# Attention scores on four 64x64 tiles of the array, and the gate sums moved four steps forward

## The chip, the cores and the metric

The kernel runs on one core of a Trainium2 chip. A core has a matrix engine (TensorE; PE in the profile, with PEld for its weight loads), a vector engine (VectorE, DVE), a scalar engine (ScalarE, ACT), a general engine (GpSimd, POOL) and a queue engine that issues transfers (SyncE, SP). Each has its own instruction stream, and they wait for each other by semaphores. Matrix products read the on-chip memory and write to accumulator banks (PSUM, eight banks of 128 partitions x 512 f32), which VectorE and ScalarE read. The metric is device time in microseconds (us), the median of several executions.

## The reference

Multi-query attention (8 batches, 16 heads, 384 tokens, head size 64, one key and value head) is followed by a mixture of experts over the 3072 tokens: each token picks one of 4 groups and then one of 4 experts in that group.

```python
scores = scale * np.matmul(q, k.transpose(0, 1, 3, 2))
scores = scores - np.max(scores, axis=-1, keepdims=True)
attn = np.exp(scores)
attn = attn / (np.sum(attn, axis=-1, keepdims=True) + 1e-09)
x = np.matmul(attn, v)            # as (3072, 1024) for what follows
...
g_idx = np.argmax(x @ w_group, axis=1)       # g_w: its softmax weight
e_idx = np.argmax(xg @ w_expert[g], axis=1)  # e_w: its softmax weight
h = np.maximum(xg[mask_e] @ w1[g, e], 0.0)
out[tok_idx] = (g_w * e_w)[:, None] * (h @ w2[g, e])
```

## The kernel before

**Tiling and loop.** The attention is cut into 24 tiles t (batch b = t // 3, token tile j = t % 3 of 128 tokens). A tile has eight units, one for each pair of heads, and the main loop takes two units in each of its 96 steps i, four steps to a tile (p = i % 4). The program's order in this loop is the order on each engine's queue; nothing reorders it later.

**A step.** `scores` (L194 to L202) computes for a unit the 128 x 384 scores of two heads: the transposed queries `qt` hold one head in partitions 0 to 63 and the other in 64 to 127, the transposed keys `kt` hold the same keys in both halves, and for each head one f32 matmul with 64 rows and 128 weight columns writes one bank of the unit's PSUM tile `s` (two banks; two such tiles exist, so the unit after the next one needs the bank back). `soft` (L204) takes the negated row maximum on VectorE (`nmx`, L209, one instruction for both heads) and the exponentials with their row sums on ScalarE (L212, one per head). Then TensorE has other work: in steps p = 0 and 1 a share of the expert's matmuls (`advance`, L553; first layer L465, second layer L479), in steps p = 2 and 3 half each of the previous tile's product with V (`pv`, L238, matmul at L249). `pv` cuts the array into 32-row by 64-column tiles: for each of 12 key blocks and four row groups, two heads, with heads as the column half (`tile_position=(32 * i, h * D)`). VectorE goes on with the 32x32 block transposes of the probabilities of two steps before (`transp`, L231), `norm` (L221) takes the reciprocals of the row sums on VectorE (L223) and multiplies the probabilities by them on GpSimd (L227): this is the scaling. In some steps VectorE also transposes queries (`q_blocks`, L186) and keys (`k_blocks`, L165).

**Slots of a step.** Further work is entered by `at(step, where, function)` (L564) and run at named places of that step (L634 to L660): "m0", "m1" and "m2" around TensorE's other work, "v" after it, "w" after the transposes and right before `norm`, "e" right after `norm`, "g" at the step's end.

**The gate.** For each batch, the logits are computed in steps 12b+8 and 12b+16 (`logits`, L266). In step 12b+9 the first token tile chooses the expert that gets the whole batch (`gate_first`, `gate_choose` with the matmul of L333, `gate_score` from L342, `gate_pick` from L362), and the loads of its weights are issued from GpSimd (`load_main`, L445). `gate_masks` (L303, step 12b+17) makes the choice of every token and the exponentials `g_ex`. `gate_values` (L400) then sums these exponentials and takes the reciprocals on VectorE (L402, L404) and makes the weights on GpSimd with four small products (L407, L411, L419, L423). `gate_selected` (L429) reduces them to one factor per token (`gsel`, L433, VectorE). The expert of batch b (`main_expert`, L517) is spread over the steps from 12b+17 on, and reads `gsel` when its second layer's results are scaled (L497), first in step 12b+24.

**After the loop** (L664 to L732) the last tile's product, the last batch's expert and a second expert for that batch follow; the steps of the last batch that lie beyond 95 are run there by hand (`run(i + 10, "w")` and so on, with i = 96). A loop over further experts, as many as remain, comes last (L734).

Of the kernel before, what the change touches and what calls it, by code (L numbers as in the profile page):

```python
# [12 lines left out]
P = 128  # L13
# [6 lines left out]
def kernel(  # L20
# [11 lines left out]
    nc = tc.nc  # L32
    B, H, S, D = q.shape
# [160 lines left out]
    def scores(u):  # L194
        b, j, c = units[u]
        qt, kt = st["qt", u // 8, c // 4], st["kt", b]
        s = ps_s.tile([P, 2, 512], FP32, tag="s")
        cc = c % 4
        for h in range(2):
            r = slice(h * D, (h + 1) * D)  # L200
            nc.tensor.matmul(out=s[:, h, 0:S], lhsT=qt[r, ts(cc, P)], rhs=kt[r, :], start=True, stop=True)  # L201
        st["s", u] = s  # L202

    def soft(us, between):  # L204
# [359 lines left out]
    def at(slot, where, fn, *args):  # L564
        later.setdefault((slot, where), []).append((fn, args))

    def run(slot, where):
        for fn, args in later.pop((slot, where), []):
            fn(*args)
# [4 lines left out]
    for b in range(B):  # L574
        s0 = SB * b
        for x, j0, j1 in ((s0 + 8, 0, 1), (s0 + 16, 1, ST)):
            at(x, "m2", logits, b, j0, j1)
            at(x + 1, "v", logits_out, b, j0, j1)
        at(s0 + 9, "v", gate_first, b)
        at(s0 + 9, "m2", gate_choose, b)  # L580
        at(s0 + 9, "w", gate_score, b)
        at(s0 + 9, "w", gate_pick, b)
        at(s0 + 9, "g", load_main, b, 0)
        at(s0 + (10 if b == B - 1 else 9), "g", load_main, b, 1)
        at(s0 + 16, "g", keep_xb, b)
        at(s0 + 17, "v", gate_masks, b)
        x = s0 + (19 if b == B - 2 else 22)
        at(x, "w", gate_values, b)
        at(x + 1, "w", gate_selected, b)
        if b == B - 1:  # L590
            at(s0 + 13, "w", gate_pick_second, b)
        if b + 1 < B:
            at(s0 + 2, "g", load_k, b + 1)
            at(s0 + 4, "g", load_v, b + 1)
            at(s0 + 7, "g", scale_k, b + 1)
            at(s0 + 8, "e", k_blocks, b + 1)
# [17 lines left out]
    for g in range(G):  # L614
        nc.sync.dma_start(
            out=wge[:, :, G + g * Eg:G + (g + 1) * Eg],
# [17 lines left out]
    for i in range(NSL):  # L634
        t, p = i // 4, i % 4
        if i >= SB + 5 and (i - 5) % SB == 0:
            pending.append(main_expert((i - 5) // SB - 1, lambda k: True))
        us = (2 * i, 2 * i + 1)
        for u in us:
            scores(u)  # L640
        run(i, "s")
        soft(us, lambda: run(i, "b"))
        if p < 2:
            run(i, "m0")
            advance(1)
            run(i, "m1")
            advance(2 if p == 1 and t % ST > 0 else 1)
        elif t > 0:
            pv(t - 1, (p - 2) * NB // 2, (p - 1) * NB // 2)
        run(i, "v")  # L650
        run(i, "m2")
        if i >= 2:
            transp(2 * i - 4)
            transp(2 * i - 3)
        run(i, "w")
        norm(us)
        run(i, "e")
        if p == 3 and t > 0:
            pv_out(t - 1)
        run(i, "g")  # L660
# [3 lines left out]
    b = B - 1  # L664
    i = NSL
# [30 lines left out]
        out=low, in_=low, pattern=[[-1, P]], compare_op=ALU.is_gt, fill=0.0, base=0, channel_multiplier=1  # L696
# [17 lines left out]
        out=sel[:], in0=iop, scalar1=pcum[:, 0:1], scalar2=pw[:, 0:1], op0=ALU.is_equal, op1=ALU.mult  # L714
# [10 lines left out]
    nsum = pool.tile([P, 1], FP32, tag="r_ns", bufs=1)  # L725
    nc.vector.tensor_reduce(out=nsum[:], in_=fl, axis=AX.X, op=ALU.add)
    nc.vector.tensor_copy(out=lsi[:, NP:NP + 1], in_=nsum[:])
    run(i + 10, "w")
    run(i + 11, "w")
    assert not later  # L730

    advance(1000)  # L732
# [2 lines left out]
    with tc.For_i(0, n_rem, 1) as it:  # L735
        free.clear()
        e = nc.gpsimd.value_load(lse[0:1, ds(it, 1)], min_val=0, max_val=GE - 1)
# [4 lines left out]
            out=xr[:].rearrange("p c t -> p (c t)"), in_=xb_dram[ds(bi, 1)].rearrange("o p c -> (o p) c")  # L742
# [43 lines left out]
```

## Time and profile before

| | us |
|---|---|
| median of 3 runs | 533.39 |
| lowest and highest run | 532.93, 533.71 |
| the profiled execution's own time | 532.0 |
| its span on the core | 530.6 |
| TensorE busy in the span | 504.5 |
| VectorE busy | 416.0 |
| ScalarE busy | 319.6 |
| GpSimd busy | 284.5 |

The granted clock of TensorE was 0.99 in the mean. The rows that the prediction quotes are of four kinds. The page's first part gives each engine's busy time, its share of the span and its instructions. The page's chain follows the work that ended last back from the end, and gives the share of the span by engine and by line. A timeline row has start and length in us, engine, line, operation, written and read tiles, shape of the tile on the array (rows * columns), sizes and count; a row can merge several instructions that follow each other, and in brackets stands the idle time of the engine before it and what ended it ("issue" means that the profile shows nothing it waited for). A list of durations has a line's instructions with the shortest, median and longest in ns. An f32 matmul leaves two matmul records and two weight loads.

### The profile page before, as it was taken

To read this page: it belongs to the slowest core of one execution; us is meant where nothing else is said; L and a number is where in the kernel's file an instruction comes from. 1 tells how busy PE (TensorE), PEld (TensorE's weight loads), DVE (VectorE), ACT (ScalarE), POOL (GpSimd) and SP (SyncE) were. 2 spreads that over 40 slices of the span, in tenths; PEclk is the share of its full clock that TensorE was granted. 3 is DMA by queue.
4 is the path that set the end of the run, shared out by engine and by line. 5 is a ranking of instruction groups with operands and counts; after the bars stand their busy time and mean duration, and the time that the engine had idled before them with its cause. 6 is when DMAs were issued, how large, how long until landed. Compare 5 with 4: busy or idle time off the path is not lost.

```text
span 530.6 us, 18457 instructions
## 1 busy us (share of the span) xinstructions
PE 504.5 (95%) x7470; PEld 283.0 (53%) x7470; DVE 416.0 (78%) x751; ACT 319.6 (60%) x997; POOL 284.5 (54%) x505
## 2 busy tenths in 40 slices
PE   7787899999999999999999999999999999999993
PEld 3254456545565556546655556545664555655451
DVE  3889988998799879987979878987899888914221
ACT  3776776676576667577666666676757666623210
POOL 1555965575458546675349456665458546704000
PEclk9799999999999999999999999999999999999998
DMA  8521996499937993599837993699739950599923
GB/s 112 118 40 43 178 242 159 75 191 246 249 76 124 225 267 89 98 210 252 209 72 134 230 262 76 117 218 241 192 72 172 236 162 3 84 234 259 212 57 94
DMA packets 65607, 83.96 MB, mean 158 GB/s; under 512 B 21232, under 2 KB 40688, under 8 KB 65520
## 3 DMA queue, kind: packets, MB, share of 16 engines
q0 software_dynamic: 19008, 37.75, 39.7%
q1 hardware_dynamic: 45024, 44.65, 33.2%
q8 instruction: 60, 0.98, 0.7%
q10 hardware_dynamic: 1488, 0.36, 0.4%
q14 instruction: 27, 0.22, 0.1%
HBM read 101.61 MB, written 18.87 MB: 227 GB/s over the span
## 4 chain that ended last, share of the span: by engine, by line
PE 84%; DVE 8%; ACT 5%; issue 2%; ACTq 0%; DVEq 0%
PE s L201 22%; PE x L249 22%; PE x L465 14%; PE x L479 12%; PE sb L479 6%; ACT pr L212 5%; PE sb L465 4%; DVE nmx L209 4%; PE x L272 2%; DVE ring L233 2%; DVE qt L191 1%; PE x L98 1%; DVE ohs_all L365 0%; DVE rinv L223 0%; DVE im L367 0%
## 5 line engine op out<-in xcount | busy, mean ns | idle before, releaser
L227 POOL TENSOR_SCALAR pr<-pr,rinv 128x384 f32<-128x384 f32 x384 | 217.1, 583 | 159.7 <-DVE rinv L223 159.7
L212 ACT ACTIVATE pr<-s,nmx 128x384 f32<-128x384 f32 x384 | 217.7, 579 | 139.5 <-DVE nmx L209 134.2
L209 DVE TENSOR_REDUCE nmx<-s 128x2 f32<-128x768 f32 x192 | 174.4, 947 | 50.8 <-PE s L201 50.4
L233 DVE STREAM_TRANSPOSE ring<-pr 128x768 f32<-128x768 f32 x192 | 175.3, 952 | 0.0
L201 PE MATMUL s<-kt,qt 64*128 64x384 f32 x768 | 157.1, 521 | 12.2 <-ACT pr L212 12.0
L249 PE MATMUL x<-ring,v_sb 32*64 32x256 f32 x4608 | 139.5, 379 | 1.6 <-issue 1.5
L249 PEld LDWEIGHTS x<-ring,v_sb 32*64 32x64 f32 x4608 | 102.1, 131 | 43.2 <-issue 24.7
L201 PEld LDWEIGHTS s<-kt,qt 64*128 64x128 f32 x768 | 65.4, 188 | 74.8 <-ACT pr L212 40.0
L465 PEld LDWEIGHTS <-w 128*128 128x128 bf16 x576 | 54.5, 98 | 46.0 <-issue 11.4
L212 ACT ACTIVATION_READ_ACCUMULATOR pr<-s,nmx 128x1 f32 x384 | 77.8, 203 | 0.0
L465 PE MATMUL x<-xb,w 128*128 128x384 bf16 x448 | 76.5, 327 | 0.0
L479 PEld LDWEIGHTS <-h_t 128*128 128x128 bf16 x432 | 40.6, 98 | 56.6 <-issue 10.6
L479 PE MATMUL x<-w,h_t 128*128 128x512 bf16 x288 | 65.3, 380 | 0.0
L263 ACT COPY xt<-x 128x256 f32<-128x256 f32 x96 | 29.0, 386 | 7.3 <-PE x L249 7.3
L479 PE MATMUL sb<-w,h_t 128*128 128x512 bf16 x144 | 31.8, 379 | 0.0
L264 POOL CAST xb<-xt 128x1024 bf16<-128x1024 f32 x24 | 24.8, 1033 | 12.8 <-ACT xt L263 12.8
L471 ACT ACTIVATE h_t<-x 128x384 bf16<-128x384 f32 x56 | 25.4, 502 | 6.1 <-PE x L465 3.3
L440 POOL DMA_DIRECT2D w<-in_moe_w_dram x36 | 27.9, 787 | 2.0 <-issue 2.0
L497 ACT ACTIVATE y<-x,gsel 128x512 f32<-128x512 f32 x36 | 25.0, 693 | 3.9 <-PE x L479 3.9
L191 DVE STREAM_TRANSPOSE qt<-q_sb 128x512 f32<-128x512 f32 x38 | 26.1, 688 | 0.0
L465 PE MATMUL sb<-xb,w 128*128 128x384 bf16 x128 | 21.4, 326 | 0.0
L223 DVE RECIPROCAL rinv<-ssum 128x4 f32<-128x4 f32 x96 | 13.6, 141 | 3.1 <-ACT pr L212 3.1
(85 smaller groups left out, 138.3 us busy)
## 6 DMA issues: line engine op xcount, KB each, us to landing
w<-in_moe_w_dram POOLq DMA_DIRECT2D x36, 1024.0 KB, 18.1
q_sb<-in_q_dram SPq DMA_DIRECT2D x76, 224.0 KB, 6.2
out_dram<-y SPq DMA_DIRECT2D x84, 128.0 KB, 6.4
xb_scratch<-xb SPq DMA_DIRECT2D x8, 768.0 KB, 4.4
v_sb<-in_v_dram SPq DMA_DIRECT2D x32, 96.0 KB, 3.5
kk<-in_k_dram SPq DMA_DIRECT2D x28, 92.0 KB, 3.7
q_sb<-in_q_dram SPq DMA_DIRECT2D x16, 128.0 KB, 3.5
out_dram<-y SPq DMA_DIRECT2D x24, 64.0 KB, 1.7
```

What stands on the lines that cost most here:

```text
L191: nc.vector.transpose(out=qt[:].rearrange("p (x d) -> p x d", d=32), in_=q_sb[:, :, 0:32])
L201: nc.tensor.matmul(out=s[:, h, 0:S], lhsT=qt[r, ts(cc, P)], rhs=kt[r, :], start=True, stop=True)
L209: nc.vector.tensor_reduce(out=nmx[:], in_=s[:, :, 0:S], axis=AX.X, op=ALU.max, negate=True)
L212: nc.scalar.activation(out=pr[:, h, :], in_=s[:, h, 0:S], func=ACTF.Exp, bias=nmx[:, h:h + 1], scale=1.0, accum_out=ssum[:, k, h:h + 1],)
L227: nc.gpsimd.tensor_scalar(out=pr, in0=pr, scalar1=rinv[:, k, h:h + 1], scalar2=1.0, op0=ALU.mult, op1=ALU.mult)
L233: nc.vector.transpose(out=ring[:, (u // 4) % 3, u % 4].rearrange("p h s -> p (h s)"), in_=st.pop(("pr", u))[:].rearrange("p h s -> p (h s)"),)
L249: nc.tensor.matmul(out=o[i][h * D:(h + 1) * D, 0:2 * P].rearrange("d (g c q) -> d g c q", g=2, c=4), lhsT=v_sb[r, n, :], rhs=ring[r, a:z + ...
L263: nc.scalar.copy(out=xt[:, :, ts(i, 32)], in_=o[:, 0:2 * P].rearrange("p (c q) -> p c q", c=KO))
L440: nc.gpsimd.dma_start(out=w[:, o:o + 4, :], in_=(w1f, w2f)[n][ds(e, 1), :, o:o + 4, :].rearrange("o p c f -> (o p) c f"))
L465: nc.tensor.matmul(out=hp[:, 0:S], lhsT=w1[:, ko, ts(fc, P)], rhs=xb[:, ko, :], start=(ko == 0), stop=(ko == KO - 1))
L471: nc.scalar.activation(out=h_t[:, fc, :], in_=hp[:, 0:S], func=ACTF.Relu)
L479: nc.tensor.matmul(out=yp, lhsT=h_t[:, fo, ts(j, P)], rhs=w2[:, fo, ts(nh, 512)], start=(fo == 0), stop=(fo == FO - 1),)
```

## The change

The score matmul of each head is cut by tokens into two of 64 weight columns each, with the array position written out: four tiles of 64 rows by 64 columns, one for each head and each half of the 128 tokens. They write the same banks as before, the token halves into partitions 0 to 63 and 64 to 127.

`gate_values` moves from slot "w" of step 12b+22 (12b+19 for the last batch but one) to slot "e" of step 12b+18, so from ahead of `norm` to behind it and four steps (one step) forward. `gate_selected` moves from step 12b+23 (12b+20) to step 12b+22 (12b+19), its slot "w" unchanged. After the loop, the last batch's two calls follow the same order as before under other names.

```diff
         for h in range(2):
             r = slice(h * D, (h + 1) * D)
-            nc.tensor.matmul(out=s[:, h, 0:S], lhsT=qt[r, ts(cc, P)], rhs=kt[r, :], start=True, stop=True)
+            for m in range(2):
+                nc.tensor.matmul(
+                    out=s[m * D:(m + 1) * D, h, 0:S], lhsT=qt[r, ts(2 * cc + m, D)], rhs=kt[r, :],
+                    start=True, stop=True, tile_position=(h * D, m * D),
+                )
         st["s", u] = s
...
-        x = s0 + (19 if b == B - 2 else 22)
-        at(x, "w", gate_values, b)
-        at(x + 1, "w", gate_selected, b)
+        x = s0 + 18
+        at(x, "e", gate_values, b)
+        at(s0 + (19 if b == B - 2 else 22), "w", gate_selected, b)
...
+    run(i + 6, "e")
     run(i + 10, "w")
-    run(i + 11, "w")
     assert not later
```

## The prediction

> **What bounds the kernel now.** I read the page first: busy shares, then the chain that ended last.
>
> ```profile
> span 530.6 us, 18457 instructions
> PE 504.5 (95%) x7470; PEld 283.0 (53%) x7470; DVE 416.0 (78%) x751; ACT 319.6 (60%) x997; POOL 284.5 (54%) x505
> ...
> PE 84%; DVE 8%; ACT 5%; issue 2%; ACTq 0%; DVEq 0%
> PE s L201 22%; PE x L249 22%; PE x L465 14%; PE x L479 12%; PE sb L479 6%; ACT pr L212 5%; PE sb L465 4%; DVE nmx L209 4%; PE x L272 2%; DVE ring L233 2%; DVE qt L191 1%; PE x L98 1%; DVE ohs_all L365 0%; DVE rinv L223 0%; DVE im L367 0%
> ```
>
> A chain that is TensorE for 84% says that TensorE's own sequence sets the end, and the scores of L201, which the change rewrites, hold 22% of it. Next the timeline of one steady slot, a step of the main loop (here step 43, whose second half is a quarter of the products with V):
>
> ```profile
> 202.91 1.56 PE L201 MATMUL s<-kt,qt 64*128 64x384 f32 x8
> 203.87 1.82 DVE L209 TENSOR_REDUCE nmx<-s 128x2 f32<-128x768 f32 x2 [0.61 <-PE s L201]
> 204.40 2.85 PE L249 MATMUL x<-ring,v_sb 32*64 32x256 f32 x96
> 204.92 0.58 ACT L212 ACTIVATE pr<-s,nmx 128x384 f32<-128x384 f32 x1 [1.88 <-DVE nmx L209]
> 205.61 1.83 DVE L233 STREAM_TRANSPOSE ring<-pr 128x768 f32<-128x768 f32 x2
> 207.17 1.56 PE L201 MATMUL s<-kt,qt 64*128 64x384 f32 x8
> 207.36 0.14 DVE L223 RECIPROCAL rinv<-ssum 128x4 f32<-128x4 f32 x1
> ```
>
> TensorE goes from scores (1.49 us to the next group) to the products with V (2.77 us) and straight on to the next scores: a period of 4.26 us with no wait. VectorE idles 0.61 us in it, waiting for the scores; ScalarE idles 1.88. So what TensorE loses in a score group is lost to the kernel, and only that.
>
> Now the inside of the score group, from narrow windows of the same timeline, each listing the instructions that touch it:
>
> ```profile
> 202.55 0.42 PE L249 MATMUL x<-ring,v_sb 32*64 32x256 f32 x8
> 202.91 0.59 PE L201 MATMUL s<-kt,qt 64*128 64x384 f32 x2
> 203.33 0.81 PE L201 MATMUL s<-kt,qt 64*128 64x384 f32 x4
> 203.98 0.49 PE L201 MATMUL s<-kt,qt 64*128 64x384 f32 x2
> 204.40 0.42 PE L249 MATMUL x<-ring,v_sb 32*64 32x256 f32 x1
> ```
>
> and the duration lists of the two lines:
>
> ```profile
> L201 PEld LDWEIGHTS s<-kt,qt x768: 182/186/335, 7.2 to 457.8; 64*128 64x128 f32 x192
> L201 PE MATMUL s<-kt,qt x768: 482/482/1007, 7.2 to 458.2; 64*128 64x384 f32 x192
> L249 PEld LDWEIGHTS x<-ring,v_sb x4608: 127/132/132, 31.4 to 476.4; 32*64 32x64 f32 x192
> L249 PE MATMUL x<-ring,v_sb x4608: 371/374/426, 31.4 to 476.7; 32*64 32x256 f32 x192
> ```
>
> Each f32 matmul leaves two records (768 for 384 matmuls). The two heads already run side by side, in pairs, on the upper and lower 64 rows of the array. Four pairs, starting at 202.91, 203.33, then 0.32 later, then 203.98, and the next group at 204.40. A pair streams for 0.32 us. The first step is 0.42, and its matmuls last 0.59 instead of 0.482: **0.105 us of the weight load is uncovered**, because nothing precedes it in this tile shape. The last step is 0.42 too: 0.09 until another tile shape may start.
>
> **The change part by part.** *Streaming: nothing.* Each score matmul becomes two with 64 weight columns each and the same 384 moving columns; 8 matmul records per slot become 16, four abreast instead of two. Four waves of 0.32 us remain, provided the four tiles run together. The products with V show that they can: eight tiles of 32*64, two of them side by side over the same rows, start within one wave (the row at 202.55: 8 records in 0.42 us, one lasting 0.374, so 0.0066 us apart).
>
> *Uncovered weight load: 0.054 us less a slot.* The first load of 64 columns lasts 127 ns against 182 for 128 columns (minima above), and the first V matmul after a change of shape lasts 0.425 against 0.374, an uncovered 0.051 against 0.105. Both differences say 0.054.
>
> *Stagger: 0.013 back.* The fourth tile of a wave starts three steps of 0.0066 after the first, where the second started one step after it; both the next shape and VectorE's maximum (L209) wait for the last. Net **0.041 us a slot**, the same for the wait of VectorE. Bounds: 0.054 (no stagger) and about 0 (below, if loads over the same rows queue up).
>
> *Change of shape: kept.* The row pairs
>
> ```profile
> 77.11 4.07 PE L465 MATMUL x<-xb,w 128*128 128x384 bf16 x24
> 81.12 1.56 PE L201 MATMUL s<-kt,qt 64*128 64x384 f32 x8
> ```
>
> give the price where the rows alone change (128*128 to 64*128). The records last 0.326, so 24 in 4.07 are 0.163 apart, the last starts at 80.86, and the scores start 0.26 after it: 0.09 more than a step. Into and out of the V shape it is 0.09 as well. From 64*64 to 32*64 the rows alone change too, so I keep 0.09 each way; the other bound is 0.
>
> *How many slots give it.* The chain has 22.2% of 530.6 = 118 us on L201, or 79 whole groups of 1.49 us; pieces of a group on the chain carry the uncovered load as well, so between 79 and 96 slots; I take 84, nearer to the lower end, since whole groups are what the steady rows show. 84 x 0.041 = **-3.4 us** (bounds 0 and 84 x 0.054 = 4.5).
>
> *Gate sums and products: nothing.* The stretch in which they stand today, and which loses time:
>
> ```profile
> 217.47 0.17 PE L333 MATMUL x<-first,ones 128*128 128x16 bf16 x1
> 217.70 0.17 DVE L342 SCALAR_TENSOR_TENSOR scr<-x,tie 128x16 f32<-128x16 f32 x1 [0.35 <-PE x L333]
> 219.61 1.78 DVE L209 TENSOR_REDUCE nmx<-s 128x2 f32<-128x768 f32 x2
> 221.91 0.92 PE L201 MATMUL s<-kt,qt 64*128 64x384 f32 x4
> 222.31 0.58 ACT L212 ACTIVATE pr<-s,nmx 128x384 f32<-128x384 f32 x1
> 223.03 0.92 PE L201 MATMUL s<-kt,qt 64*128 64x384 f32 x4 [0.21 <-ACT pr L212]
> 223.06 0.17 DVE L402 TENSOR_REDUCE es<-g_ex 128x15 f32<-128x60 f32 x1
> 223.27 0.25 DVE L404 RECIPROCAL wt<-es 128x15 f32<-128x15 f32 x1
> 223.43 0.12 DVE L223 RECIPROCAL rinv<-ssum 128x4 f32<-128x4 f32 x1
> 223.47 1.79 DVE L209 TENSOR_REDUCE nmx<-s 128x2 f32<-128x768 f32 x2
> ```
>
> In step 47 the second score unit waits until 223.03 for the exponentials of step 46 (last one ends 222.89), and these were late because VectorE, held by the choice of experts (L342 from 217.70), reached their maxima only at 219.61. L402 and L404 come after that, at 223.06: 0.4 us of VectorE that TensorE's wait does not contain. Moved to step 42 behind its scaling they fall, with 0.42 us, into the 0.61 us of idle at 203.87 (0.57 with the shorter scores), so they cost nothing there; without that cover it would be 0.42 for each of 7 batches, 2.9 us. The four GpSimd products (L407 to L423), now behind the scaling instead of ahead of it, wait for nothing and issue no DMA; no queue is passed. The gate column sum (L433) goes one step forward, before its first reader still. After the loop both calls keep their order.
>
> The wait in this stretch does swallow the saving of step 46; that is one slot in each of six batches, inside the 96 to 84.
>
> *Supply of instructions: +0.4 us.* Some V groups are longer than 2.85 us:
>
> ```profile
> 183.67 3.46 PE L249 MATMUL x<-ring,v_sb 32*64 32x256 f32 x96
> 262.62 2.82 PE L249 MATMUL x<-ring,v_sb 32*64 32x256 f32 x88
> 266.11 0.66 PE L249 MATMUL x<-ring,v_sb 32*64 32x256 f32 x8 [0.67 <-issue]
> 418.89 3.48 PE L249 MATMUL x<-ring,v_sb 32*64 32x256 f32 x96
> 475.93 1.11 PE L249 MATMUL x<-ring,v_sb 32*64 32x256 f32 x27 [0.88 <-issue]
> ...
> q8 instruction: 60, 0.98, 0.7%
> ```
>
> The excesses are 0.61, 1.30 (262.62 to 266.77), 0.63 and 0.88, 3.4 us together. TensorE waits for nothing that the profile shows; V groups consume instructions fastest (192 in 2.8 us), and 60 packets of 16 KB bring them. The change adds 8 weight loads and 8 matmuls a slot, 1536 to 14940: 10% more packets, so I add 10% of the 3.4 and a little for smaller ones, 0.4 us. Where the packet borders then fall I cannot tell: some of four to seven stalls may vanish or come, +-2 us.
>
> The Trainium skill (Runtime: NRT & Kernel Launch, "Instruction fetch mechanics") has an engine refill in blocks of 256 instructions, the crossing "mostly hidden"; by it this term would be 0. The rows above disagree with "hidden" in the V groups.
>
> **Sum.** -3.4 + 0.4 = -3.0 us against the profiled execution's own 532.0 (span 530.6 plus 1.4): 529.0. The median of the runs shown, 533.39, stands 1.4 above that execution, so I forecast **530.4**.
>
> **Rivals.** *The stalls grow (slower).* Place: V groups, where a packet border falls into a run that consumes 192 instructions in 2.8 us. If a third of the 46 V groups in the loop stalled by the middle excess, 0.62, that is 15 x 0.62 = 9.3 in place of 3.4: +5.9 - 3.4 = +2.5, **535.9**. It decides from 3.4 us of new stalls on. For it: 10% more instructions, 16 more right ahead of every V group. Against it: score groups still consume slowly (32 in 1.45 us).
>
> *The four tiles do not run together (slower).* If the second column half of a row half starts only when the first has streamed, each slot has eight waves instead of four: 4 x 0.32 = 1.28 us, 90 slots, +115: about **646**. Against it stands the V wave at 202.55, two column halves over the same rows within 0.007 us. A rule speaks for it: the Trainium skill (TensorE: Matmul & The Clock Gate, Part 3, "The mechanism") lets a weight load overlap a running matmul only in another row group, and the new halves share theirs. The V wave disagrees.
>
> *No gain.* If only the loads over the same rows queue, the uncovered load stays 0.105 while the stagger grows; or VectorE, 78% busy, takes over as the bound: about **533.8**.
>
> *The changes of shape go away*, as both shapes now have 64 columns: 46 V groups x 2 x 0.09 = 8.3 more, **522**. Against it the rows-only change above.
>
> *The gate move pays* 0.4 in 7 batches, **527.5**; against it the order of events at 222.89 and 223.06.
>
> **How the numbers follow.** Forecast 0.70, more stalls 0.08, no tiles together 0.04, no gain 0.08, no change of shape 0.04, gate move 0.06. About 0.2%, 1.1 us, is what a measurement of this kernel tells from no change. Around the forecast the stalls' +-2 us leave 0.59 faster, 0.10 within, 0.01 slower; the cheaper rivals add 0.10 to faster, no gain adds 0.07 to the same, the stalls and the serial tiles 0.11 to slower: 0.69, 0.18, 0.13. The likeliest case alone spans 527.8 to 533; reaching to the gate move below and to no gain above gives 527.0 to 534.0.
>
> **What would show it.** Right: 1536 matmul records on the score line of 64*64, first ones near 0.53 us, median still 0.482, four starts within 0.02 us; a score group 1.45 us to the next; shape changes still 0.09; VectorE's idle after the moved gate sums near 0.15. The step after the choice of experts still waits for ScalarE. Wrong: score waves at 0.64, a first matmul still at 0.59, or idle "issue" ahead of or inside V groups well over the 3.4 us counted here.

## The result and the profile after

The changed kernel takes 525.55 us (median of 4 runs, 524.93 to 526.60) against 533.41 before: ratio 0.9855, interval 0.9836 to 0.9875. Measured again beside the experiments it took 526.06 against 534.62, ratio 0.9861 (0.9838 to 0.9884). The gain is 7.9 us; 3.0 were forecast. One of the four executions of the run scores_only below took 1269.3 us; its time there is the median of the other three.

The page of the changed kernel (its lines behind the score matmul lie 4 or 5 below the old ones: L202 is the score matmul, L253 the product with V, L406 and L408 are the gate sums):

```profile
span 523.5 us, 19997 instructions
...
PE 494.6 (94%) x8238; PEld 263.9 (50%) x8238; DVE 416.1 (79%) x751; ACT 319.7 (61%) x997; POOL 285.5 (55%) x505
...
PEclk9999999999999999999999999999999999999997
...
q8 instruction: 66, 1.08, 0.8%
...
PE 83%; DVE 8%; ACT 6%; issue 2%; ACTq 0%; DVEq 0%
PE x L253 22%; PE s L202 21%; PE x L469 14%; PE x L483 12%; PE sb L483 6%; ACT pr L216 5%; PE sb L469 4%; DVE nmx L213 4%; PE x L276 2%; DVE ring L237 2%; DVE qt L191 1%; PE x L98 1%; DVE ohs_all L369 0%; DVE im L371 0%; DVE rinv L227 0%
```

TensorE still carries the chain. It has 768 more matmuls (and as many weight loads) and is busy for 10 us less. The timeline of the same step 43:

```profile
199.93 1.52 PE L202 MATMUL s<-kt,qt 64*64 64x384 f32 x16
200.22 0.14 DVE L227 RECIPROCAL rinv<-ssum 128x4 f32<-128x4 f32 x1
200.27 0.18 DVE L406 TENSOR_REDUCE es<-g_ex 128x15 f32<-128x60 f32 x1
200.49 0.25 DVE L408 RECIPROCAL wt<-es 128x15 f32<-128x15 f32 x1
200.88 1.82 DVE L213 TENSOR_REDUCE nmx<-s 128x2 f32<-128x768 f32 x2
201.38 2.85 PE L253 MATMUL x<-ring,v_sb 32*64 32x256 f32 x96
```

A score group now takes 1.45 us to the next group (199.93 to 201.38), against 1.49. The gate sums lie in VectorE's former idle time and leave 0.14 of it (200.74 to 200.88). The narrow windows of this group and the durations of the line:

```profile
199.58 0.42 PE L253 MATMUL x<-ring,v_sb 32*64 32x256 f32 x8
199.93 0.55 PE L202 MATMUL s<-kt,qt 64*64 64x384 f32 x4
200.31 0.83 PE L202 MATMUL s<-kt,qt 64*64 64x384 f32 x8
200.95 0.50 PE L202 MATMUL s<-kt,qt 64*64 64x384 f32 x4
201.38 0.43 PE L253 MATMUL x<-ring,v_sb 32*64 32x256 f32 x1
```

```profile
L202 PEld LDWEIGHTS s<-kt,qt x1536: 129/133/133, 6.7 to 450.6; 64*64 64x64 f32 x192
L202 PE MATMUL s<-kt,qt x1536: 479/482/534, 6.7 to 450.9; 64*64 64x384 f32 x192
```

Four tiles start together (four records in 0.55 us, the longest 0.534). The first step is 0.38 instead of 0.42, the waves stay 0.32 apart, and the change of shape still costs its 0.43 after the last wave, so 0.1 beyond a step. Each of these was forecast.

**Where the 7.1 us of the span went.** I compared the two traces step by step, from the first score matmul of a step to that of the next. Of the 96 steps, 68 are shorter by 0.04 us, -2.7 together; with six more in which a stall hides it, -3.0. In six steps the kernel before lost time inside V or score groups to waits for nothing visible, and the changed kernel does not: -3.3. In steps 15 to 17 the changed kernel has one such wait of its own, +1.1:

```profile
65.45 0.87 PE L202 MATMUL s<-kt,qt 64*64 64x384 f32 x7
67.07 1.12 PE L202 MATMUL s<-kt,qt 64*64 64x384 f32 x9 [0.76 <-issue]
```

Steps 0 and 3 to 5 are shorter by 1.4, and the first score matmul starts 0.5 earlier. The page of before has a slower clock there (its second slice, 13 to 27 us):

```profile
PEclk9799999999999999999999999999999999999998
```

The rest is +0.1, behind the loop. So the weight load is 3.0 of 7.1, and the largest other term is the missing stalls. The experiments ask why they are missing.

The clock explains little of the 7.9 us between the medians. Of 79 executions of the kernel before, measured beside the experiments, 29 have a mean granted clock of 0.993 or more; their median is 533.42. Seven of the ten executions of the changed kernel have such a clock; their median is 525.89, still 7.5 less.

**What the stalls have in common.** The page of before lists 60 instruction packets, 0.98 MB; counting TensorE's records in the trace in order gives 15,200, or 253 to a packet; after the change it is 16,740 to 66, or 254. The Trainium skill (Runtime: NRT & Kernel Launch, "Instruction fetch mechanics") gives 256 instructions to a block, and the trace agrees. In the count, four of the waits of before come right behind records 5312, 7872, 12736 and 14528: each is 192 above a multiple of 256. I call such a place a border. From the first score matmul of a batch to that of the next, the trace of the kernel before has 1854 TensorE records (batches 2 to 6), and the changed one 2047: 192 more weight loads and matmuls and one more semaphore instruction. The second count is 8 x 256 - 1, where the expectations below have 7 x 256 + 1; both are one off a whole number of packets. In the changed kernel, then, the borders come to almost the same place of the program in every batch, one record later each time; before, 1854 = 7 x 256 + 62 moved them by 62 records in each batch.

### The profile page after: what moved, and what is told of

Read it like the earlier page. It is cut to its first block, busy times and chain, and to the rows that moved or that the text cites. A ratio compares the mean times of both kernels' runs of the same rounds, so it can differ in the third digit from the quotient of the medians.

```text
span 523.5 us, 19997 instructions
## 1 busy us (share of the span) xinstructions
PE 494.6 (94%) x8238; PEld 263.9 (50%) x8238; DVE 416.1 (79%) x751; ACT 319.7 (61%) x997; POOL 285.5 (55%) x505
## 4 chain that ended last, share of the span: by engine, by line
PE 83%; DVE 8%; ACT 6%; issue 2%; ACTq 0%; DVEq 0%
PE x L253 22%; PE s L202 21%; PE x L469 14%; PE x L483 12%; PE sb L483 6%; ACT pr L216 5%; PE sb L469 4%; DVE nmx L213 4%; PE x L276 2%; DVE ring L237 2%; DVE qt L191 1%; PE x L98 1%; DVE ohs_all L369 0%; DVE im L371 0%; DVE rinv L227 0%
## 5 line engine op out<-in xcount | busy, mean ns | idle before, releaser
L202 PE MATMUL s<-kt,qt 64*64 64x384 f32 x1536 | 150.5, 497 | 15.5 <-ACT pr L216 14.2
L253 PE MATMUL x<-ring,v_sb 32*64 32x256 f32 x4608 | 137.0, 378 | 1.3 <-issue 1.3
L253 PEld LDWEIGHTS x<-ring,v_sb 32*64 32x64 f32 x4608 | 101.4, 131 | 43.6 <-issue 23.7
L202 PEld LDWEIGHTS s<-kt,qt 64*64 64x64 f32 x1536 | 47.6, 132 | 86.6 <-ACT pr L216 50.1
```

The costliest lines, as they stand in the source:

```text
L202: nc.tensor.matmul(out=s[m * D:(m + 1) * D, h, 0:S], lhsT=qt[r, ts(2 * cc + m, D)], rhs=kt[r, :], start=True, stop=True, tile_position=(h ...
L253: nc.tensor.matmul(out=o[i][h * D:(h + 1) * D, 0:2 * P].rearrange("d (g c q) -> d g c q", g=2, c=4), lhsT=v_sb[r, n, :], rhs=ring[r, a:z + ...
```

## The experiments

Ratios are to the kernel before, measured with each group of runs.

| run | us | ratio, interval |
|---|---|---|
| gates_only | 534.55 | 1.000, 0.997 to 1.003 |
| scores_only | 526.93 | 0.985, 0.980 to 0.989 |
| after_pad32 | 527.19 | 0.990, 0.986 to 0.994 |
| after_pad224 | 529.92 | 0.995, 0.990 to 0.999 |
| after_pad64 | 532.47 | 0.996, 0.994 to 0.998 |
| after_pad146 | 537.96 | 1.008, 1.005 to 1.012 |
| after_drift | 534.02 | 1.000, 0.997 to 1.004 |
| tiles_64x32 | 543.88 | 1.020, 1.016 to 1.023 |
| before_noload | 533.71 | 1.000, 0.998 to 1.002 |
| after_noload | 531.19 | 0.996, 0.994 to 0.998 |
| pad146_noload | 534.11 | 1.002, 0.999 to 1.005 |
| after_again | 526.06 | 0.986, 0.984 to 0.988 |

**Each part alone.** The gate move without the score tiles (the old line 201 back in the changed kernel):

```diff
-            for m in range(2):
-                nc.tensor.matmul(
-                    out=s[m * D:(m + 1) * D, h, 0:S], lhsT=qt[r, ts(2 * cc + m, D)], rhs=kt[r, :],
-                    start=True, stop=True, tile_position=(h * D, m * D),
-                )
+            nc.tensor.matmul(out=s[:, h, 0:S], lhsT=qt[r, ts(cc, P)], rhs=kt[r, :], start=True, stop=True)
```

> The kernel before with the gate sums, products and column sums moved as in the change, scores on 64x128 as before. The number of TensorE instructions stays that of before. Theory (the gate move is worth nothing, the 7.9 us come from the scores, half of them from where the 256-instruction packets end in the V groups): 533.4, within 0.2%, V groups with the same excesses at about the same steps. Rival (the gate move pays 0.4 us in each of 7 batches): 530.5.

534.55, ratio 1.000: the gate move is worth nothing that can be told from no change, and the 2.9 us of the rival lie outside the interval. The stalls stay (about 7 us in steps 18 to 94 of its profile, against 3.3 in that of before); they are not the same in each execution. The timeline of step 79, which had none in the profile of before:

```profile
382.60 1.10 PE L249 MATMUL x<-ring,v_sb 32*64 32x256 f32 x26
384.53 2.38 PE L249 MATMUL x<-ring,v_sb 32*64 32x256 f32 x70 [0.83 <-issue]
```

The score tiles without the gate move (the same hunk put into the kernel before):

> The kernel before with the scores on four 64x64 tiles, gate work in its old place. Theory: all of the change, 525.6 (ratio 0.985), no V group of the main loop from step 16 on longer than 2.85 us. Rival (the gate move carries a part): about 528.5.

526.93, ratio 0.985: all of the change, within the interval. Its profile has two late V groups (0.78 and 0.36 us over, steps 19 and 55), so "none" was too strong.

**Moving the borders.** Tiny matmuls in the first four steps, where TensorE waits, shift every later border and leave the rest alone:

```diff
+    def pad(n):
+        x = xbank()
+        for _ in range(n):
+            nc.tensor.matmul(out=x[0:32, 0:16], lhsT=blank[:, 0:32], rhs=blank[:, 0:16], start=True, stop=True)
...
         soft(us, lambda: run(i, "b"))
+        if i < 4:
+            pad([18, 18, 18, 19][i])
```

> The changed kernel with 73 tiny matmuls (128x32 weights of zeros, 16 columns) spread over the first four steps, where TensorE waits anyway: 146 more instructions, so that every later packet border falls 146 instructions earlier in the program, modulo 256. One batch of the changed kernel has 7 x 256 + 1 TensorE instructions, so the borders come to nearly the same place in each batch. Now they lie 7 to 88 instructions into a V group and no group stalls; with the shift they lie at about 122 and 158 in the second V group of two tiles of each batch, where the kernel before stalled by 0.4 to 1.3. Theory (the place of the border decides): 11 to 15 us slower than the changed kernel, 537 to 540, with V groups of 3.2 to 4.1 us in the same two steps of every batch. Rival (the stalls went because the score groups now give the instruction supply more time, or by chance of the transfers): 525.6, as the changed kernel.

537.96, 12 us slower than the changed kernel, as the border theory said and the rival did not. In the profiles 11.3 us of this lie in steps 18 to 94, far behind the padding. The timeline of its V groups in steps 27, 39 and 75, the same step of three batches:

```profile
125.55 1.97 PE L258 MATMUL x<-ring,v_sb 32*64 32x256 f32 x60
128.14 1.51 PE L258 MATMUL x<-ring,v_sb 32*64 32x256 f32 x36 [0.62 <-issue]
...
185.31 1.97 PE L258 MATMUL x<-ring,v_sb 32*64 32x256 f32 x61
187.91 1.51 PE L258 MATMUL x<-ring,v_sb 32*64 32x256 f32 x35 [0.62 <-issue]
...
364.20 1.98 PE L258 MATMUL x<-ring,v_sb 32*64 32x256 f32 x62
366.79 1.45 PE L258 MATMUL x<-ring,v_sb 32*64 32x256 f32 x34 [0.62 <-issue]
```

The reader should compare the counts. The group breaks after 60, 61 and 62 matmuls, that is, after 120 to 124 records with the weight loads, and the borders counted in the trace lie at 121, 124 and 133. The two drift apart because this trace lacks 16 matmul records (8295 against 8311 weight loads), so that the count runs more and more short. The break itself comes about one record later in each batch, as 2047 says. It breaks in all six batches from step 27 on, by 1.05 to 1.25 us. Only one of the two forecast steps stalls in its V group; the other part of the loss (0.4 to 0.9) is in the step behind it.

The same padding with eight matmuls a step:

> The changed kernel with 32 such tiny matmuls in the first four steps: 64 more instructions, borders then lie 80 instructions ahead of a V group to 24 into it. Theory: no stalls in the steady steps, 525.6; up to 2 us less if the single stall at step 15 and the one behind the loop go. Rival (the padding itself costs): over 526.5.

532.47: the expectation was wrong. No V group from step 16 on is late, as said, but I had reckoned with borders in V groups alone. They now fall into the score group behind them (steps 28 and 40):

```profile
127.84 0.86 PE L207 MATMUL s<-kt,qt 64*64 64x384 f32 x5
129.22 1.50 PE L207 MATMUL s<-kt,qt 64*64 64x384 f32 x11 [0.52 <-issue]
...
187.00 0.86 PE L207 MATMUL s<-kt,qt 64*64 64x384 f32 x5
188.05 1.50 PE L207 MATMUL s<-kt,qt 64*64 64x384 f32 x11 [0.18 <-issue]
```

That group follows two V groups that have used up the instructions just as fast. Six batches lose 0.5 to 1.4 us each there. Two smaller shifts, by 32 either way (4 and 28 matmuls a step):

> The changed kernel with 16 tiny matmuls (32 instructions) in the first four steps. Borders come 32 instructions earlier: at most 53 into a V group, and 236 behind the start of the second V group of a batch's first tile, past the score group in which the shift by 64 stalled. Theory (place decides): no stalls from step 16 on, 524 to 526. Rival (any shift away from the changed kernel's own place costs): 528 or more.

> The changed kernel with 112 tiny matmuls (224 instructions, so a shift by 32 the other way). Borders at about 45, 80 and 117 in the second V groups of a batch's three tiles. Theory: the first two are below the 105 from which the kernel before stalled, and the third tile never stalled there: 525 to 528. Rival: 530 or more.

527.19 is a little over the range, 529.92 too: with the second, V groups with borders 43 to 46 and 77 to 83 matter already (0.5 and 0.9 us over), where I had put the limit at 105. The order of the five shifts, 0, 32, 224, 64, 146, is the order of what their profiles lose in steps 18 to 94 (0, 0.6, 4.2, 7.1 and 11.3 us over the changed kernel's). Of the four other places tried, the shift by 32 cost 1.6 us and the rest 4 to 12.

**Setting the borders in motion.** Not shifted once, but by 32 instructions in each batch, with matmuls inside a wait:

```diff
         for u in us:
             scores(u)
+            if u % 2 == 0 and i > SB and i % SB == SB - 1:
+                for _ in range(16):
+                    nc.tensor.matmul(
+                        out=st["s", u][0:D, 0, S:S + 16], lhsT=blank[0:D, 0:D], rhs=blank[0:D, 0:16],
+                        start=True, stop=True, tile_position=(0, 0),
+                    )
```

> The changed kernel with 16 tiny matmuls (64x64 tiles of zeros, 16 columns, into unused columns of the score tile) between the two score units of step 12b+11, b >= 1, where TensorE waits about 0.4 us for ScalarE. 32 more instructions a batch: the borders no longer come to the same place but move 32 a batch, through all places in eight batches. The matmuls lie in a wait, so they should cost under 0.1 us a batch. Theory (the change is worth its 3 us of weight load, and the rest is that its borders stand still at a good place): some batches stall, 3 to 6 us over the changed kernel, 528.5 to 531.5. Rival (the stalls went because of the lighter score groups): 525.6 to 526.3.

534.02, the time of before, so the whole gain is gone, and more than expected. The steps with the added matmuls are as long as in the changed kernel (within 0.06 us); the loss, 7.0 us between steps 18 and 94, lies almost wholly in nine other steps of six batches, such as step 51:

```profile
242.56 2.81 PE L253 MATMUL x<-ring,v_sb 32*64 32x256 f32 x86
245.80 0.67 PE L253 MATMUL x<-ring,v_sb 32*64 32x256 f32 x10 [0.43 <-issue]
```

So with borders that wander in this way the changed kernel is no faster than the kernel before: waits for instructions take back what the score tiles save in weight load.

**Smaller tiles still.** Eight score tiles of 64x32 (`for m in range(4)`, 32 columns each):

> The changed kernel with eight score tiles of 64x32 in place of four of 64x64. Theory of the weight load: the uncovered load falls again by half, 0.053 to 0.027 us, and the stagger grows from 3 to 7 steps of 0.0066: first matmuls near 0.51 us, a score group 1.45 us to the next group, as with four tiles, so nothing from this term. A batch then has 7 x 256 + 385 instructions, so the borders take two places in turn, half a packet apart: stalls in about half of the batches, 2 to 6 us over the changed kernel. Rival (streaming time depends on the tiles): a group well off 1.45 us.

Durations of its score line, and step 43 of the timeline:

```profile
L202 PE MATMUL s<-kt,qt x3072: 479/482/508, 7.1 to 470.1; 64*32 64x384 f32 x192
```

```profile
207.63 1.52 PE L202 MATMUL s<-kt,qt 64*32 64x384 f32 x32
209.08 3.29 PE L253 MATMUL x<-ring,v_sb 32*64 32x256 f32 x96
```

The weight-load arithmetic holds: first matmuls of 0.508, a group of 1.45 us. The sum of the stalls does not: 16.4 us over the changed kernel between steps 18 and 94, not 2 to 6. A batch has 2428 records here, 9 x 256 + 124 (the trace lacks a few), so the borders do take two places in turn; they cost far more than was thought, and the kernel takes 543.88.

**The packets themselves.** The traces also keep when each packet of queue q8 started and how long it took, and this settles what the stalls wait for. A packet lands at its start plus that time. In steps 18 to 94 the 14 traces of this document have 45 gaps of 0.5 us or more between the starts of two TensorE instructions, inside a V or score group, that no semaphore explains; eleven of the traces have at least one. Each gap ends 1.2 to 1.6 us after a packet has landed, and each lies at a border, as far as missing records let one count. Three of them, and the same step of the changed kernel without a stall (us from the start of the span):

| run, step | the border before | packet starts | it lands | TensorE goes on at the border | gap |
|---|---|---|---|---|---|
| before, 55 | 259.95 | 263.43 | 264.84 | 266.11 | 1.04 |
| after_pad146, 27 | 122.47 | 125.95 | 126.94 | 128.14 | 0.99 |
| after_noload, 43 | 198.75 | 201.70 | 203.10 | 204.54 | 0.93 |
| after, 43 | 197.22 | 198.72 | 200.31 | 201.89 | none |

The changed kernel has 52 borders in these steps, and at every one the packet had landed at least 1.35 us before TensorE came to it. So each of these stalls is the wait for a packet that landed too late. The place of a border in its V group alone does not decide: in the kernel before, borders 155 and 163 records into a V group (steps 26 and 74) cost nothing. What counts is the time that TensorE leaves from one border to the next, 4.7 us where both fall into neighbouring V groups (steps 42 and 43 of the changed kernel), and how soon after the first the packet starts.

**What makes a packet late.** In these three, batches 1 to 6 use the first batch's expert weights:

```diff
+    w_first = []
+
     def load_main(b, n):
+        if 0 < b < B - 1:
+            st["w", b] = w_first
+            return
...
+        if b == 0:
+            w_first.append(st["w", b][-1])
```

> The kernel before without the weight loads of batches 1 to 6: these batches use the first batch's expert weights (left out: 24 of 36 weight loads, so the outputs of these batches are of another expert). TensorE's instructions stay. Theory (an instruction packet comes late when it queues behind the weight loads): the stalls of the V groups between steps 24 and 90 go, 3 to 4 us less than the kernel before, 529.5 to 531. Rival (a packet takes that long by itself): stalls as before, 533.5.

> The changed kernel without the same weight loads. Theory: it had no stalls in these steps, so 525.5 to 526; and against the kernel before without these loads the difference is the weight-load term of the forecast alone, 3 to 4 us. Rival (the score tiles give 8 us by themselves): 8 us less than the kernel before without these loads.

> The changed kernel with the 146 instructions of padding, without the same weight loads. Theory: the stalls of 1.2 us in step 12b+15 and 0.7 in the step behind it go for the batches without loads, about 9 to 12 us less than with the loads, 526 to 529. Rival (the border's place alone decides, whatever the transfers do): 538, as with the loads.

533.71, 531.19 and 534.11: the theory, that packets queue behind the weight loads, is half right at best. In step 12b+15 the stalls do go. The V group of step 39 in pad146_noload, 1.25 us late with the loads, is at its 2.85 again:

```profile
184.23 2.85 PE L258 MATMUL x<-ring,v_sb 32*64 32x256 f32 x96
```

But new ones come in step 12b+19 (31, 43 and so on to 79), also in the changed kernel, which had none there. Step 43 of after_noload:

```profile
201.44 1.52 PE L202 MATMUL s<-kt,qt 64*64 64x384 f32 x16
202.89 1.09 PE L253 MATMUL x<-ring,v_sb 32*64 32x256 f32 x24
204.54 2.39 PE L253 MATMUL x<-ring,v_sb 32*64 32x256 f32 x72 [0.56 <-issue]
```

The break is after 24 matmuls, and the border counted there is 51. The packets show the exchange: with the padding, the one for step 39 starts 3.3 us after the border before it with the loads and 1.6 without, the one for step 43 starts 1.7 after it with the loads and 3.4 without. Taking away two thirds of the weight loads made the changed kernel 5.6 us slower. What sets the start of a packet is not settled; what is shown is that the transfers shift the late starts and with them the stalls, and that fewer transfers do not remove them.

**The changed kernel once more.**

> The changed kernel unaltered, in as many rounds and on such chips as the experiments, to set them against. Theory (its packet borders lie at a good place whatever the chip): ratio 0.985 to the kernel before again, a profile without a stalled V group from step 16 to 95. Rival (the first profile was a lucky one, its transfers happened to come in time): ratio 0.99 or more, with stalls of 0.4 to 1.3 us in some batches.

Ratio 0.986. One V group is late in the profile (0.37 us, step 19), none in the other batches: the near absence of stalls is not the luck of one execution. It is not complete either, as scores_only, with the same TensorE instructions, shows.

## Why the prediction was right and where it was wrong

- *Streaming and tiles together*: right. Four records start within one wave, and the median matmul stays at 0.482.
- *Uncovered weight load less stagger, 0.041 a step*: right; 0.040 in 68 steps and under the stalls of six more. So the number of steps was 74 and not 84, since early steps and those behind the choice of experts, which wait for VectorE and ScalarE, gave nothing: 3.0 instead of 3.4.
- *Change of shape kept*: right, 0.1 either way as before.
- *Gate move worth nothing*: right; gates_only is at 1.000. VectorE's idle is 0.14 where 0.15 was forecast, and the step behind the choice of experts still waits for ScalarE.
- *Supply of instructions, +0.4 us, "some of four to seven stalls may vanish or come, +-2 us"*: this is the step that failed. It added 10% for 10% more packets and treated the stalls as separate accidents. They are not: a batch of 2047 instructions is one less than eight packets, so the borders stay where they are and the batches tend to stall together or not at all. Here almost none did, and the term was -3.3 in the steady steps and +1.1 at step 15, together -2.2 in place of +0.4 and outside the stated 2 us. That the place is a good one is luck; nothing in the change aims at it, and the same kernel shifted by 146 instructions pays 12 us. The count needed for this, instructions of a batch against the size of a packet, could be made before the run: 192 is the diff's own number and 1854 was in the trace. What the place would cost could not be read from it.
- *The rival "the stalls grow"* had the place and the price per stall right (0.62 and more, V groups), and is what the change does under another shift.
- Some 1.9 us more of the span, the start and steps 0 to 5, were in no term. The clock row shows a slower slice there in the profile of before. It belongs to that execution more than to the change: at equal clock the medians still differ by 7.5 us, and half clock in some of the first 50 us stands also in traces of runs with the score tiles, such as after_drift and after_noload.
- *The size of the miss*: 525.55 is 4.9 below the forecast. The supply term is 2.6 of it and the early steps 1.9; the weight load gave 0.4 less than forecast; the last 0.8 is that the medians differ by 7.9 us and the two profiled spans by 7.1. The kernel before stalls by a different amount in each execution, and its profiled one, 532.0, was a quick one.

## What to carry to other kernels

A row "issue" inside a run of many small matmuls is time like any other: count the instructions from one such gap to the next, and compare the count of one loop round with the packet size. When a change alters the number of instructions of a long stream, its measured gain contains the shift of the packet borders; pad the stream by a few dozen instructions, in two or three sizes, before crediting the change. Cutting matmuls into more tiles saves uncovered weight load by the column, 0.04 us a group here with four tiles and no more with eight, and pays in instructions.

## What was not expected of the hardware

A stream of weight loads and matmuls 14 ns apart (192 records in 2.8 us) outran the instruction supply by up to 2.0 us a border (step 75 with 64x32 tiles), while the borders of the changed kernel, 11 to 88 records into such a run, cost nothing in its steady steps. In every gap of 0.5 us or more TensorE went on 1.2 to 1.6 us after the packet had landed. The Trainium skill's "mostly hidden" (Runtime: NRT & Kernel Launch, "Instruction fetch mechanics") fits the changed kernel's steady steps, but not the run with 64x32 tiles, which lost 16 us. And a kernel became slower, 525.6 to 531.2, when 24 of its 36 weight loads were taken away.
